# One mask pass and one r-by-decay pass for both chunks in units 0 to 8, the mix as two products of halves, and the opening in another order

## The chip, the core and the metric

The kernel runs on one core of one Trainium2 chip. The metric is the device time of one execution in microseconds (us). TensorE multiplies matrices, VectorE and ScalarE work element by element from SBUF or PSUM, GpSimd from SBUF alone, and SyncE issues the DMAs. In the views they are PE (PEld is its weight load), DVE, ACT, POOL and SP.

## The reference

Three stages follow each other. The first is a recurrence over time with one 48 by 48 state for each of 8 heads, for 4 batches of 768 steps. The second and third are two dense networks on the 3072 tokens that come out.

```python
for t in range(S):
    cur = einsum('bhd,bhe->bhde', u * k[t], v[t])
    y[t] = einsum('bhd,bhde->bhe', r[t], state + cur)
    state = w[t][..., None] * state + einsum('bhd,bhe->bhde', k[t], v[t])
x = y as 3072 x 384
h = x @ w_in;  x = (h * sigmoid(1.702 * h)) @ w_out          # 384 -> 2048 -> 384
h = x @ w_in2; s = h * softmax(h); x = layernorm(s) * g @ w_out2   # 384 -> 1024 -> 384
```

## The kernel before

**Units.** The recurrence is cut into 24 units (`NU`), six for each batch (`UB`), each of 128 time steps in two chunks of 64 (`C`). In a unit, rows 64 to 111 of the tile `rkw` hold chunk 0's 48 channels and rows 0 to 47 hold chunk 1's, for all heads side by side. The decays' running products are `P` (`f_scan`, token `F1`); `f_back` (`F3`) forms their inverses, and `f_k` (`F5`) multiplies them into k. `f_r1` (`F2` on GpSimd, `FV` on VectorE) multiplies r by the decay for chunk 1's rows into a tile R1, and `f_r0` (`FG` on GpSimd) does so for chunk 0's rows into R0.

**One unit on TensorE.** `scores` (`SA`) makes k times r within each chunk, 64 by 64 for each head: 16 products. `masked` (`M0`, `M1`) multiplies each chunk's scores by a triangular mask into the free half of R0 and R1. So R0 holds masked scores and decayed r one above the other, and `mix` (`X`) needs one product for each head and half chunk: 32 products, each 32 columns of weights wide, four of them beside each other, with v and the carried state stacked in the same way in `vs0` and `vs1`. `turn_k` (`ST`) and `copy_k` (`SK`) turn k, and `states` makes k times v. With tokens `DA`, `DB` it is added to the old state on TensorE by identity products, chunk by chunk; with `D` it stands alone, and `update` (`U1`, `U2`) adds on VectorE. A star at a token means the form on TensorE. `bonus`, `bonus_sum` and `bonus_mul` (`B`, then `BS`/`BR`, then `BV`/`BW`/`BX`) make the term with u; `total` (`V`) adds it. `turn`, `out_hi`, `out_lo` (`T`, `O`, `OL`) put the unit's output into the high and low parts that the dense stage reads.

**Banks.** A unit's PSUM is three banks of one set. In units 0 to 5 the scores fill bank 1, and the mix overwrites it. In units 6 to 8 scores of two half sets of heads lie in banks 2 and 0, the turned k in bank 1, and the mix in the rest of banks 2 and 0. Later units do as units 6 to 8, with the mix in bank 1.

**The dense stage and the order.** The first network's 16 weight slices come in as 64-bit numbers and are narrowed and split into a high and a low part (tokens `Lw`, `N0`, `N1` or `NA`, `N2`, `H`, `C`; `N1` is a VectorE shift and `NA` the same on ScalarE). `h`, `e`, `g`, `o` are rise, gelu, rest and fall of one token block and one slice: `h` and `o` are 9 products each, `h0`, `o0`, `h1`, `o1` of 256 tokens, `h9` and `o9` of 512. The order of everything in units 0 to 8 is the table `START`, written out by hand and run under a manual schedule, so that each engine takes its instructions in the table's order. From unit 9 on, the lists `ENTRY`, `BYPE` and `LONG` say which steps of a unit go behind which slice of the dense stage. After all 24 units the second network follows.

Of the kernel before, what the change touches and what calls it, by code (L numbers as in the profile page):

```python
# [990 lines left out]
```

## Time and profile before

| | us |
|---|---|
| median of 3 runs (lowest, highest) | 699.23 (696.68, 701.11) |
| profiled execution, its own time | 696.9 |
| its span, first to last instruction | 695.1 |
| TensorE busy in the span | 675.5 |
| VectorE, ScalarE, GpSimd busy | 516.7, 326.0, 151.2 |
| TensorE's last product of `START` ends, unit 9's `turn_k` begins | 134.35 |

The granted TensorE clock reads 1.00 in the whole span. A busy time is the union of an engine's instructions. Of TensorE's the ends are modelled, so a busy stretch can still hold short waits. The part of the span that the change touches is its first fifth: up to 134 us for units 0 to 8, and the handover to unit 9 behind it.

### The profile page before, as it was taken

What the parts mean: (1) busy time and instruction counts of PE and PEld (TensorE: products, weight loads), DVE (VectorE), ACT (ScalarE), POOL (GpSimd) and SP (SyncE); (2) the same over time, 40 slices, a digit from 0 to 9 for tenths busy, and PEclk for the clock granted to TensorE, in tenths of its full rate; (3) what the DMA queues carried; (4) which work ended last, traced back from release to release, by engine and by line L of the source; (5) the groups of instructions that cost most, each with busy time, mean ns of one, the idle gap of its engine ahead of it and who ended that gap; (6) DMA issues with size and microseconds to landing.
All of it is one profiled execution on the core that took longest, in us unless ns stands there. A gap on an engine that the chain in (4) does not pass through costs nothing.

```text
span 695.1 us, 15308 instructions
## 1 busy us (share of the span) xinstructions
PE 675.5 (97%) x6015; PEld 570.9 (82%) x6015; DVE 516.7 (74%) x815; ACT 326.0 (47%) x726; POOL 151.2 (22%) x146
## 2 busy tenths in 40 slices
PE   3899999999999999999999999999999999999997
PEld 2679878778888888888878888888899989999997
DVE  7898998898797777677777422566688888878872
ACT  4578985532334332432242224565655555455552
POOL 7555124332322222222123200120000000000000
PEclk9999999999999999999999999999999999999999
DMA  8696734545545455455453121340245444444443
GB/s 306 205 347 232 251 110 130 183 136 152 150 144 149 136 151 152 141 144 144 133 148 97 51 90 37 101 135 25 75 149 175 144 170 149 148 156 156 153 149 106
DMA packets 70872, 102.75 MB, mean 148 GB/s; under 512 B 16016, under 2 KB 55440, under 8 KB 70800
## 3 DMA queue, kind: packets, MB, share of 16 engines
q1 hardware_dynamic: 70656, 101.68, 46.0%
q8 instruction: 47, 0.77, 0.5%
q14 instruction: 25, 0.20, 0.1%
q10 hardware_dynamic: 144, 0.10, 0.0%
HBM read 77.82 MB, written 23.92 MB: 146 GB/s over the span
## 4 chain that ended last, share of the span: by engine, by line
PE 91%; DVE 3%; DMA 2%; ACT 2%; issue 1%; POOL 1%; SPq 0%; ACTq 0%; DVEq 0%; POOLq 0%
PE acc L628 26%; PE h L603 26%; PE o L739 14%; PE right L671 8%; PE left L671 7%; PE att L369 2%; DMA rk<-in_rkw 1%; PE att L279 1%; PE att L370 1%; PE d L525 1%; DVE xTl L420 1%; PE att L313 0%; PE att L317 0%; PE att L240 0%; PE att L306 0%
## 5 line engine op out<-in xcount | busy, mean ns | idle before, releaser
L628 PE MATMUL acc<-gh,w 128*128 128x512 f32 (+1 forms) x606 | 198.4, 384 | 0.0
L603 PE MATMUL h<-xTh,w 128*128 128x512 f32 (+1 forms) x606 | 164.9, 381 | 0.3 <-DVE gl L618 0.3
L611 ACT ACTIVATE gh<-h 128x512 fp32r<-128x512 f32 (+1 forms) x101 | 58.0, 575 | 212.6 <-PE h L603 211.0
L618 DVE TENSOR_TENSOR gl<-h,gh 128x512 fp32r<-128x512 f32 (+1 forms) x101 | 66.4, 659 | 87.3 <-ACT h L613 86.6
L628 PEld LDWEIGHTS acc<-gh,w 128*128 128x128 f32 x606 | 112.4, 188 | 22.5
L603 PEld LDWEIGHTS h<-xTh,w 128*128 128x128 f32 x606 | 110.0, 188 | 22.1 <-DVE gl L618 0.5
L628 PE MATMUL acc<-gl,w 128*128 128x512 f32 (+1 forms) x303 | 114.9, 379 | 0.0
L603 PE MATMUL h<-xTl,w 128*128 128x512 f32 (+1 forms) x303 | 82.4, 380 | 0.5 <-DVE xTl L420 0.5
L739 PE MATMUL o<-w,qh 128*128 128x384 f32 x384 | 70.9, 336 | 0.0
L739 PEld LDWEIGHTS o<-w,qh 128*128 128x128 f32 x384 | 67.7, 188 | 1.6
L603 PEld LDWEIGHTS h<-xTl,w 128*128 128x128 f32 x303 | 55.2, 188 | 12.4 <-DVE xTl L420 1.8
L628 PEld LDWEIGHTS acc<-gl,w 128*128 128x128 f32 x303 | 57.0, 188 | 10.1
L613 ACT ACTIVATE h<-h 128x512 f32<-128x512 f32 (+1 forms) x101 | 57.8, 572 | 0.0
L716 POOL TENSOR_TENSOR sm<-sm,mhalf 128x1 f32<-128x1 f32 x24 | 13.2, 549 | 199.0 <-DVE sm L715 177.6
L229 POOL TENSOR_TENSOR vd<-vd,dg 128x384 f32<-128x384 f32 x16 | 17.4, 1086 | 153.8 <-DMA vd<-in_vn 122.2
L173 POOL TENSOR_TENSOR R<-rk,P 64x512 f32<-64x512 f32 x22 | 29.0, 1317 | 73.9 <-PE att L370 42.2
L671 PE MATMUL right<-w,x2h 128*128 128x512 f32 x156 | 39.9, 391 | 0.0
L291 DVE TENSOR_TENSOR R<-att,cc 64x256 f32<-64x256 f32 (+1 forms) x82 | 36.8, 448 | 1.9 <-PE att L273 0.9
L739 PE MATMUL o<-w,ql 128*128 128x384 f32 x192 | 37.1, 334 | 0.0
L202 POOL TENSOR_TENSOR nr<-nr,nk 128x384 f32<-128x384 f32 x24 | 29.6, 1232 | 21.8 <-ACT nr L214 11.5
L188 DVE TENSOR_TENSOR_SCAN w<-w,ipc 112x520 f32<-112x520 f32 x24 | 33.5, 1397 | 0.8
L671 PE MATMUL left<-w,x2h 128*128 128x512 f32 x132 | 33.9, 392 | 0.0
(182 smaller groups left out, 1212.8 us busy)
## 6 DMA issues: line engine op xcount, KB each, us to landing
rk<-in_rkw SPq DMA_DIRECT2D x24, 512.0 KB, 4.1
d<-t SPq DMA_DIRECT2D x24, 512.0 KB, 2.6
back<-d SPq DMA_DIRECT2D x96, 128.0 KB, 2.7
x2b<-in_w SPq DMA_DIRECT2D x11, 768.0 KB, 6.0
w<-in_rkw SPq DMA_DIRECT2D x24, 261.0 KB, 3.0
nr<-in_nat SPq DMA_DIRECT2D x24, 192.0 KB, 2.9
nk<-in_nat SPq DMA_DIRECT2D x24, 192.0 KB, 2.9
vs<-in_vn SPq DMA_DIRECT2D x48, 96.0 KB, 4.1
```

The source lines that it names most:

```text
L173: (e or self.nc.gpsimd).tensor_tensor(out=heads(R1[0:64]), in0=heads(s["rkw"][0:64, 0:HC]), in1=heads(s["P"])[0:64, :, 0:C], op=ALU.mult)
L188: v.tensor_tensor_scan(out=w[:, n:0:-1], data0=w[:, n:0:-1], data1=self.ipc[:, n:0:-1], initial=0.0, op0=ALU.mult, op1=ALU.add)
L202: g.tensor_tensor(out=s["nr"], in0=s["nr"], in1=s["nk"], op=ALU.mult)
L229: g.tensor_tensor(out=heads(s["vd"]), in0=heads(s["vd"]), in1=dg.unsqueeze(2).to_broadcast([128, H, D]), op=ALU.mult)
L291: self.nc.vector.tensor_tensor(out=heads(R[q:q + 64])[:, h:h + n], in0=a, in1=m.unsqueeze(1).to_broadcast([64, n, C]), op=ALU.mult)
L603: nc.tensor.matmul(out=h_ps, lhsT=W1[f][:, ws + c * 128:ws + (c + 1) * 128], rhs=xs[:, c, tok], start=n == 0, stop=n == 8)
L611: nc.scalar.activation(out=gh, in_=h_ps, func=AF.Gelu_apprx_sigmoid)
L613: return nc.scalar.activation(out=h_ps, in_=h_ps, func=AF.Gelu_apprx_sigmoid)
L618: nc.vector.tensor_tensor(out=gl_, in0=g, in1=gh.bitcast(F32), op=ALU.subtract)
L628: nc.tensor.matmul(out=a, lhsT=W1[f][:, ws + e * 128:ws + (e + 1) * 128], rhs=gs, start=first and n == 0, stop=last and n == 2)
L671: nc.tensor.matmul(out=h_ps[:, b * 512:(b + 1) * 512], lhsT=xs[:, c], rhs=W2I[c][wb][:, b * 512:(b + 1) * 512], start=n == 0 and c == 0, s ...
L739: nc.tensor.matmul(out=o, lhsT=(lo if n == 2 else hi)[:, f * 128:(f + 1) * 128], rhs=W2O[f][n == 1], start=n == 0 and f == 0, stop=n == 2 ...
```

## The change

For units 0 to 8 (`QUADS` is now 9) four things are different.

1. `f_r1` multiplies all 112 rows in one pass, into one tile R0; `f_r0` is no longer called there.
2. Scores of both chunks lie one above the other in bank 1, and `masked` is one pass of 128 rows into a tile R1 of its own. Units 6 to 8 leave their four-fold layout and take that of units 0 to 5. `turn_k` uses bank 0 in every unit.
3. `mix` is two steps. `within` (token `X`) multiplies the masked scores by v, 16 products of 64 rows by 64 columns of weights. `mix` (token `Y`) adds r times the carried state, 16 products of 48 by 64.
4. `START` is a new table. Unit 3's states go from the TensorE form (`DA`, `DB`, starred `U1`, `U2`) to the VectorE form. The three `N1` become `NA`. `BX`, the bonus product on ScalarE, is left in unit 6 alone (before: units 4, 5, 6, 8). Unit 9's two r passes go to VectorE. In `ENTRY` unit 9's scores come after unit 8's mix.

```diff
-QUADS = UB
 LONE = 9
+QUADS = LONE
...
-    "turn+1 copy+1 scores+1 mix rk+3 w+3 v+2 total send vd+1 fetch masks+1",
+    "turn+1 copy+1 mix scores+1 rk+3 w+3 v+2 total send vd+1 fetch masks+1",
...
     def f_r1(self, i, e=None):
+        if i < QUADS:
+            n, r = 112, self.ap.tile([112, HC], F32, tag="R0", name=f"R0_{i}", bufs=2)
+            s["R0"] = r
...
     def masked(self, i, b):
         s, q = self.st[i], 64 * b
+        if i < QUADS:
+
+            R = s["R1"] = self.ap.tile([128, HC], F32, tag="R1", name=f"R1_{i}", bufs=2)
+            self.nc.vector.tensor_tensor(out=heads(R), in0=heads(s["A"]), in1=self.mask.unsqueeze(1).to_broadcast([128, H, C]), op=ALU.mult)
+            return
...
+    def within(self, i, e=None):
+
         mm, s = self.nc.tensor.matmul, self.st[i]
+        y, M = self.bank(i, 1)[:, 0:HD], s["R1"]
...
+        for h in range(H):
+            w, d = slice(h * C, (h + 1) * C), slice(h * D, (h + 1) * D)
+            mm(out=y[0:64, d], lhsT=M[0:64, w], rhs=s["vs0"][0:64, d], start=e is None and h == 0, stop=False)
+            mm(out=y[64:128, d], lhsT=M[64:128, w], rhs=s["vs1"][64:128, d], start=e is None and h == 0, stop=False)
+
+    def mix(self, i):
+        mm, s = self.nc.tensor.matmul, self.st[i]
+        if i < QUADS:
+
+            y, R = s["y"], s["R0"]
+            for h in range(H):
+                w, d = slice(h * C, (h + 1) * C), slice(h * D, (h + 1) * D)
+                mm(out=y[64:128, d], lhsT=R[0:48, w], rhs=s["vs1"][0:48, d], start=False, stop=h == H - 1)
+                mm(out=y[0:64, d], lhsT=R[64:112, w], rhs=s["vs0"][64:112, d], start=False, stop=h == H - 1)
+            return
...
-Lrkw:0 F1:0 F3:0 F5:0 FG:0 Ln:0 FV:0 SA:0 Lcst Lb:0 ST:0 B:0 BS:0 Lrkw:1 F1:1 F2:1 FG:1 M0:0 M1:0 La:0 SK:0 DA:0 Lw:1
+Lrkw:0 Ln:0 F1:0 F3:0 La:0 F5:0 Lcst B:0 Lrkw:1 F1:1 ST:0 SK:0 Lb:0 Lw:1 F3:1 BS:0 F2:0 SA:0 M0:0 F2:1 X:0 DA:0 Lw:0
```

VectorE, unit 0 and the start of unit 1, before (`rk` is k and r, `w` the decays, `R` the tiles R0 and R1):

```order
L195 TENSOR_TENSOR rk_110<-rk_110,w_108 112x512
L173 TENSOR_TENSOR R_0_125<-rk_110,P_112 64x512
L167 SCALAR_TENSOR_TENSOR P_166<-w_162,ind 112x520
L291 TENSOR_TENSOR R_0_119<-att_85,cc 64x512
L291 TENSOR_TENSOR R_0_125<-att_85,cc 64x512
L187 RECIPROCAL ipc<-P_166 112x8
L188 SCALAR_TENSOR_TENSOR w_162<-w_162,ipc 112x520
```

The same place after the change:

```order
L199 TENSOR_TENSOR rk_110<-rk_110,w_108 112x512
L166 SCALAR_TENSOR_TENSOR P_133<-w_129,ind 112x520
L191 RECIPROCAL ipc<-P_133 112x8
L192 SCALAR_TENSOR_TENSOR w_129<-w_129,ipc 112x520
L293 TENSOR_TENSOR R_0_175<-att_85,cc 128x512
L199 TENSOR_TENSOR rk_131<-rk_131,w_129 112x512
```

Unit 0's r pass (L173) has left VectorE, both scans of unit 1 stand ahead of unit 0's mask, and the mask is one instruction.

GpSimd at the same place, before (`nr`, `nk` are the bonus term's r and k, `cc` the constants, `vd` the bonus product):

```order
L179 TENSOR_TENSOR R_0_119<-rk_110,P_112 48x512
L202 TENSOR_TENSOR nr_121<-nr_121,nk_123 128x384
L203 TENSOR_TENSOR nr_121<-nr_121,cc 128x384
L173 TENSOR_TENSOR R_1_168<-rk_164,P_166 64x512
L179 TENSOR_TENSOR R_1_170<-rk_164,P_166 48x512
```

The same place after:

```order
L206 TENSOR_TENSOR nr_112<-nr_112,nk_114 128x384
L207 TENSOR_TENSOR nr_112<-nr_112,cc 128x384
L177 TENSOR_TENSOR R_0_157<-rk_110,P_116 112x512
L177 TENSOR_TENSOR R_1_177<-rk_131,P_133 112x512
L237 TENSOR_TENSOR vd_254<-vs_0_91,dg_148 64x384
```

Unit 0's r pass now stands behind the two bonus passes, the second of which reads the constants, and each unit has one pass instead of two.

ScalarE at the end of `START`, before (`x2a` is the dense stage's stored output, `vd` the bonus product of unit 8, `kTs` unit 9's turned k):

```order
L613 ACTIVATE h_0_1803<-h_0_1803 128x512
L638 ACTIVATE x2a<-acc_79 128x512
L638 ACTIVATE x2a<-acc_80 128x512
L638 ACTIVATE x2a<-acc_79 128x512
L227 ACTIVATE vd_1774<-vd_1774,dg_1765 128x48 x8
L245 ACTIVATE kTs_1888<-att_85 128x448
```

The same place after:

```order
L631 ACTIVATE h_0_1829<-h_0_1762 128x512
L656 ACTIVATE x2a<-acc_79 128x512
L656 ACTIVATE x2a<-acc_80 128x512
L656 ACTIVATE x2a<-acc_79 128x512
L249 ACTIVATE kTs_1857<-att_84 128x448
```

Unit 8's eight bonus instructions are gone from between the stores and the copy of unit 9's turned k.

## Rows read from the trace of the kernel before

**Rows 1.** The page's part 1: busy us, share, instructions of TensorE and VectorE.

```profile
PE 675.5 (97%) x6015; PEld 570.9 (82%) x6015; DVE 516.7 (74%) x815; ACT 326.0 (47%) x726; POOL 151.2 (22%) x146
```

**Rows 2.** Stretches of `START`: length; busy PE, PEld, DVE, ACT, POOL (xcount); PEclk, DMA share, GB/s.

```profile
0.00:30.40 30.40, 17.59 (x289) 12.94 (x289) 22.30 (x29) 14.41 (x51) 19.43 (x22) 1.00 0.72 254
30.40:56.90 26.50, 25.54 (x387) 21.17 (x387) 25.16 (x34) 20.50 (x64) 17.26 (x14) 1.00 0.80 277
56.90:134.40 77.50, 77.00 (x922) 63.32 (x921) 69.63 (x104) 55.47 (x165) 25.92 (x22) 1.00 0.56 182
```

**Rows 3.** The chain of waits in order of time, 42 to 47 us: start, us, what.

```profile
42.37 1.02 ACT x2b L488
...
43.41 1.54 DVE wf L490
44.95 1.15 DVE P L167
46.10 0.46 DVE xTl L420
```

**Rows 4.** VectorE, 0 to 135 us, by line and shape: count, busy, mean ns, idle.

```profile
L618 DVE TENSOR_TENSOR gl<-h,gh 128x512 fp32r<-128x512 f32 x11 | 7.5, 686 | 0.3 <-ACT h L613 0.2
L291 DVE TENSOR_TENSOR R<-att,cc 64x512 f32<-64x512 f32 x10 | 6.9, 689 | 1.1 <-PE att L273 0.9
...
L291 DVE TENSOR_TENSOR R<-att,cc 64x256 f32<-64x256 f32 x12 | 5.1, 421 | 0.2
...
L173 DVE TENSOR_TENSOR R<-rk,P 64x512 f32<-64x512 f32 x2 | 2.1, 1073 | 0.0
```

**Rows 5.** GpSimd, 0 to 135 us, the r passes by line and shape.

```profile
L179 POOL TENSOR_TENSOR R<-rk,P 48x512 f32<-48x512 f32 x10 | 13.5, 1346 | 17.0 <-DMA nk<-in_nat 7.9 <-DVE P L167 3.9 <-DMA rk<-in_rkw 3.1
...
L173 POOL TENSOR_TENSOR R<-rk,P 64x512 f32<-64x512 f32 x8 | 11.0, 1374 | 21.7 <-DVE P L167 13.7 <-PE acc L322 5.7 <-PE att L240 2.1
```

**Rows 6.** VectorE's timeline: the same f_k pass in units 0 and 5.

```profile
6.35 1.48 DVE L195 TENSOR_TENSOR rk<-rk,w 112x512 f32<-112x512 f32 x1
...
87.11 0.69 DVE L195 TENSOR_TENSOR rk<-rk,w 112x512 f32<-112x512 f32 x1
```

**Rows 7.** TensorE's timeline: first product of a step, first of the next.

```profile
9.29 0.36 PE L273 MATMUL att<-R,rk 48*64 48x64 f32 x1 [0.91 <-DVE R L173]
...
48.22 0.53 PE L313 MATMUL att<-vs,cc 112*48 112x192 f32 x2
49.49 0.39 PE L628 MATMUL acc<-gh,w 128*128 128x256 f32 x1
...
54.19 0.23 PE L369 MATMUL att<-vs,R 112*32 112x48 f32 x1
55.01 0.38 PE L628 MATMUL acc<-gh,w 128*128 128x256 f32 x1
...
63.98 0.24 PE L305 MATMUL att<-vs,kTs 64*48 64x48 f32 x1
64.38 0.23 PE L273 MATMUL att<-R,rk 48*64 48x64 f32 x1
...
91.34 0.27 PE L272 MATMUL att<-R,rk 48*64 48x64 f32 x1
92.42 0.50 PE L628 MATMUL acc<-gh,w 128*128 128x512 f32 x1
...
102.35 0.27 PE L279 MATMUL att<-R,rk 48*64 48x64 f32 x1
102.98 0.50 PE L628 MATMUL acc<-gh,w 128*128 128x512 f32 x1
```

**Rows 8.** Timelines at the handover to unit 9: ScalarE, VectorE, TensorE.

```profile
134.55 1.58 ACT L638 ACTIVATE x2a<-acc 128x512 f32<-128x512 f32 x3 [1.69 <-PE acc L628]
...
137.94 0.56 DVE L377 TENSOR_TENSOR vd<-att,vd 128x384 f32<-128x384 f32 x1 [1.27 <-ACT vd L227]
...
153.57 0.24 PE L305 MATMUL att<-vs,kTs 64*48 64x48 f32 x1 [1.29 <-ACT kTs L261]
```

More of the change, by code (lines that the diff above doesn't have):

```diff
@@ L237, in turn_k @@
         kt, s = self.st[i]["kt"], self.st[i]
-        s["kT"] = self.bank(i, 0 if i < QUADS else 1)
+        s["kT"] = self.bank(i, 0)
         for p in range(4):
@@ L265, in scores @@
         mm, s = self.nc.tensor.matmul, self.st[i]
-        kt, R0, R1 = s["kt"], s["R0"], s["R1"]
+        kt, R0 = s["kt"], s["R0"]
         if i < QUADS:
-            A = self.bank(i, 1)
-            s["A"] = [[(A[0:64], 0, H)], [(A[64:128], 0, H)]]
+            A = s["A"] = self.bank(i, 1)
             for h in range(H):
@@ L272, in scores @@
                 mm(out=A[0:64, c], lhsT=kt[64:112, c], rhs=R0[64:112, c], start=True, stop=True)
-                mm(out=A[64:128, c], lhsT=kt[0:48, c], rhs=R1[0:48, c], start=True, stop=True)
+                mm(out=A[64:128, c], lhsT=kt[0:48, c], rhs=R0[0:48, c], start=True, stop=True)
             return
+        R1 = s["R1"]
         P, Q = self.bank(i, 2)[:, 0:4 * C], self.bank(i, 0)[:, 0:4 * C]
@@ L350, in update @@
         v.tensor_tensor(out=dst, in0=kv, in1=pc, op=ALU.mult)
-    def mix(self, i, e=None):
+    def within(self, i, e=None):
         mm, s = self.nc.tensor.matmul, self.st[i]
-        one = e is None
-        if i < QUADS or i >= LONE:
-            s["y"] = y = self.bank(i, 1)[:, 0:HD]
-            y = [y[:, h * D:(h + 1) * D] for h in range(H)]
-        else:
-            s["y"] = y = self.bank(i, 3).rearrange("p (b c) -> p b c", b=2)[:, :, 4 * C:4 * C + 4 * D]
-            y = [y[:, h // 4, (h % 4) * D:(h % 4 + 1) * D] for h in range(H)]
-        if e is not None:
-            mm(out=s["y"], lhsT=self.ident, rhs=s["vd"], start=True, stop=False)
+        y, M = self.bank(i, 1)[:, 0:HD], s["R1"]
+        s["y"] = y
+        if e is not None:
+            mm(out=y, lhsT=self.ident, rhs=s["vd"], start=True, stop=False)
+        for h in range(H):
[11 more added lines that the diff above has]
+            return
+        y = s["y"] = self.bank(i, 1)[:, 0:HD]
         for h in range(H):
@@ L786, in rwkv_moe_moe2 @@
         ST=at.turn_k, SK=at.copy_k, SA=at.scores, M0=lambda i: at.masked(i, 0), M1=lambda i: at.masked(i, 1),
-        D=at.states, DA=lambda i: at.states(i, 0), DB=lambda i: at.states(i, 1), U1=lambda i, e=None: at.update(i, 0, e), U2=lambda i, e=None: at.update(i, 1, e), X=at.mix, V=at.total,
+        D=at.states, DA=lambda i: at.states(i, 0), DB=lambda i: at.states(i, 1), U1=lambda i, e=None: at.update(i, 0, e), U2=lambda i, e=None: at.update(i, 1, e), X=at.within, Y=at.mix, V=at.total,
         T=at.turn, O=lambda i: at.out_hi(i, X), OL=lambda i, e=None: at.out_lo(i, X, e),
```

49 lines of the change are left out of this document (24 added, 25 removed).

## The prediction

> **What bounds the kernel now.** I read the page first: TensorE is busy for 675.5 of the 695.1 us [rows 1], so whatever lengthens TensorE's work late in the kernel lengthens the kernel. Then I cut `START` into stretches at two marks of the program, unit 1's turned output (30.4 us) and unit 3's (56.9 us), and read the engines in each [rows 2]. In the first 30.4 us TensorE is busy for 17.59 us only: this is a chain from engine to engine. From 30.4 to 56.9 us TensorE is busy 25.54 of 26.5 us and VectorE 25.16 us, so the two bound it together, and the chain of waits shows how: at 42 us it leaves TensorE for a weight conversion on ScalarE, a narrowing pass, a scan and an output split on VectorE, and comes back with unit 3's turn of k [rows 3]. From 56.9 to 134.4 us TensorE is busy 77.00 of 77.5 us and VectorE 69.63 us: here TensorE's work alone sets the end, and a faster VectorE or GpSimd has 0.5 us to win. After 134 us nothing of the change runs but the handover to unit 9.
>
> So the question is how much TensorE work the change adds behind 56.9 us, and how much earlier that mark is reached.
>
> **VectorE and GpSimd lose work.** A pass over 128 rows of 512 costs what one over 64 rows does: 686 ns against 689 ns [rows 4]. So the single mask pass takes about 0.69 us, and saves 0.69 us in each of units 0 to 5 and 4 x 0.42 - 0.69 = 1.0 us in each of units 6 to 8: 7.1 us in `START`, of which 2.8 us lie in the opening (units 0 to 3). Unit 0's r pass leaves VectorE as well, one of two passes of mean 1.07 us [rows 4]. Against that stand two more state additions of unit 3 and one weight shift less in the opening, all of about half a pass, which I set to nothing. VectorE has some 3.9 us less to do up to the mark. GpSimd's r passes cost 1346 ns for 48 rows and 1374 ns for 64 [rows 5], so one of 112 rows should cost about 1.36 us too, and the 18 passes before become 7. That is 15 us of GpSimd, an engine whose work lies beside others'; its worth is indirect. The f_k pass took 1.48 us in unit 0, beside a GpSimd r pass, and 0.69 us in unit 5 [rows 6].
>
> The Trainium skill (SBUF — State Buffer, section "Who interferes with whom") says that VectorE with two SBUF inputs and GpSimd share one port pair, which the first holds for its whole instruction while the other waits. The two rows of f_k agree. By the rule alone, the three GpSimd passes that go from the opening could give VectorE back up to their whole length, 3 x 1.36 = 4.1 us in place of the 0.8 us taken below, and the sum at the end would be about nothing instead of +3.2 us.
>
> I take from this row at most 0.8 us for each of three GpSimd passes that are gone from units 0 to 3, and expect a third of it, 0.8 us, since most VectorE passes of the opening are not stretched.
>
> **TensorE gains work.** The mix before takes 55.01 - 54.19 = 0.82 us for 32 products, four beside each other [rows 7]. After it is 16 products of `within` and 16 of `mix`, which can stand only two beside each other, since each covers 64 columns of weights. No row shows this form. The nearest are the scores, with the same width and places, but 64 columns moved instead of 48: 92.42 - 91.34 = 1.08 us [rows 7]. From below the old mix bounds it, whose 16 groups of two would take twice its eight groups of four in a pure count; each half then costs the whole old mix, 0.82 us. I take 0.9 us for a half, nearer to the 0.82 us because its 48 moved columns are the same. Behind the mark stand five `within` (units 4 to 8) and four `mix` (4 to 7), and before stood four old mixes: 9 x 0.9 - 4 x 0.82 = +4.8 us (4.1 to 6.4 at the ends). Unit 8's old mix and its new second half stand behind `START` alike.
>
> The scores of units 6 to 8 also go from four to two beside each other: from 102.98 - 102.35 = 0.63 us to 1.08 us [rows 7], three times: +1.35 us. The turn of unit 4's k slips behind the mark: +0.3 us. Unit 3's states lose two identity forms of 49.49 - 48.22 = 1.27 us and take one of 64.38 - 63.98 = 0.40 us [rows 7]: -2.1 us on TensorE, all ahead of the mark.
>
> **The opening.** Unit 0's first pair of scores had both r passes at 9.29 us [rows 7], because GpSimd and VectorE made one each. Now the single pass waits on GpSimd behind two bonus passes, and the second of these reads the constants, whose DMA is issued after two loads of v. I reckon its end near 11 us. TensorE turns k in the meantime, which it did afterwards before, so unit 0 loses about 1 us, not 2. What is queued behind that wait on TensorE is all of unit 0; on VectorE it is the one mask pass, with unit 1's scans already done ahead of it. Up to unit 1's turned output I see no net change: the order has then done two products' worth more (unit 2's scores, one split) in a stretch where TensorE is idle for 12.8 of 30.4 us. Between the marks TensorE has unit 3's identities and that earlier work less (-2.1 -1.1 -1.75), and four halves for two mixes more (+2.0), and one fall moved from ahead of the mark to just behind it, which I count in (+1.1): about -2 us. VectorE has about -3 us there. The two bound it together, so the mark comes 2 to 3 us earlier; I take 2.5 us. It is nothing if unit 0's delay goes through to the end, +2 us at worst, and -6 us if VectorE's 3.9 us and the stretched passes all count.
>
> **The handover.** Unit 8's total waited 1.27 us for its bonus product on ScalarE, and TensorE later 1.29 us for unit 10's k, which goes through VectorE's queue behind that total [rows 8]. The eight bonus instructions are gone, so I expect the 1.29 us to go. But unit 9's scores now need the bank of its turned k, so they wait for its copy, and this stands on ScalarE behind the stores of 1.58 us [rows 8] with only unit 8's `mix` to cover it: about +1.0 us. Together -0.3 us. The 0.5 us of idle time behind the mark may go too: -0.5 us.
>
> **Sum.** -2.5 (opening) + 4.8 (halves) + 1.35 (scores) + 0.3 (turn) - 0.3 (handover) - 0.5 (idle) = +3.2 us, since TensorE stays full behind it. The profiled execution took 696.9 us (span 695.1), 2.3 us under the median of the three runs; the sum goes 696.9 + 3.2 = 700.1 for such an execution, and 699.2 + 3.2 = 702.4 for the median.
>
> **Rivals.** *The halves do not stand beside each other.* If the two products of a pair, which read different rows and write the same bank, took turns, a half would cost twice the 0.64 us that 0.82 has without its start, 1.3 to 1.5 us: nine times +0.5 behind the mark and seven times ahead of it, where TensorE is 96% busy, so +8 us on top: 710 us. Against it: the scores write one bank from different rows and start in pairs, 1.08 us for 16. The point from which it decides is a half above 1.2 us. The Trainium skill (TensorEngine Tiling (Array Packing), section "Gotcha 1: PSUM Pressure") says that different row tiles cannot access the same PSUM bank at once, which is this rival. The scores' rows do not bear it out, so I give it one chance in ten.
>
> *The opening gives nothing.* Unit 0's r pass behind the bonus passes and the constants delays the chain by 1 to 2 us, and the order-bound queues of VectorE (a total that waits for a bonus product, with unit 1's second update behind it) keep it: 3.2 + 2.5 + 1.5 = +7.2 us, 706.4 us. For it: the first stretch is a chain with 12.8 us of idle TensorE.
>
> *The late stretch is not TensorE's.* If its busy time hides waits for VectorE, which is 90% busy there, then VectorE's 4.3 us less in masks there pay for the new products, and the +4.8 and +1.35 us fall away: 3.2 - 6.15 = -3 us, 696.2 us. Against it: the idle time there is 0.5 us.
>
> *The opening gives much more.* Units 0 to 3 reach the mark 10 us or more earlier, with all waits for conversions gone: 692 us or less. TensorE's own work up to the mark speaks against it.
>
> **Chances.** My case (698 to 706.2) 0.48; the late stretch not TensorE's (693 to 698) 0.16; the opening gives nothing 0.16, a little over half of it above 706.2; the halves apart 0.10; the opening much faster 0.10. A difference under 1%, 7 us, is about what a measurement of this kernel cannot tell from no change. So faster by over 1%: 0.10; within 1%: 0.48 + 0.16 + 0.07 = 0.71; slower by over 1%: 0.19. The range from 692.5 to 710 leaves out the fast case and half of the halves apart.
>
> **What would show it.** In the profile after: a `within` or `mix` of 0.8 to 1.1 us, pairs starting together; one mask pass of 0.69 us; first scores near 11 us; unit 3's turned output and the fall moved behind it done by 54 to 55 us; unit 9's turn of k at 137 to 139 us instead of 134.35; no wait for unit 10's k, but one of about 1 us for unit 9's scores. The prediction is wrong if unit 9's turn comes before 134 us, or if TensorE shows idle time of several us between the mark and there.

## The result and the profile after

The changed kernel takes 703.94 us (median of 18 runs, 702.27 to 708.09), the kernel before beside it 698.05 us (18 runs, 695.81 to 703.02): a ratio of 1.0094, interval 1.0073 to 1.0115. So it is 5.9 us slower by the medians, and 6.6 us by the ratio. The 18 times lie in two groups, twelve from 702.27 to 704.58 and six from 706.38 to 708.09; the profiled execution is the 702.27, with a span of 700.5 us, 5.4 more than before.

The page after, busy times, against [rows 1]:

```profile
PE 682.2 (97%) x6007; PEld 580.1 (83%) x6007; DVE 508.1 (73%) x801; ACT 323.6 (46%) x705; POOL 135.9 (19%) x140
```

TensorE has 6.7 us more, VectorE 8.6 us and GpSimd 15 us less. The windows after, cut at unit 1's turned output, at the end of the fall behind unit 3's, and at unit 9's turn of k, against [rows 2] (columns: stretch, length, busy time of each engine, granted clock, DMA share, GB/s):

```profile
0.00:30.90 30.90, 18.53 (x321) 14.74 (x321) 20.06 (x27) 16.89 (x53) 14.81 (x22) 1.00 0.82 290
30.90:56.10 25.20, 23.92 (x342) 20.84 (x343) 22.04 (x31) 19.41 (x64) 8.94 (x8) 1.00 0.82 281
56.10:140.50 84.40, 84.29 (x957) 70.74 (x956) 67.66 (x96) 53.41 (x150) 23.36 (x21) 1.00 0.49 162
```

The third row is where the time went: 84.4 us instead of 77.5, and TensorE is busy in 84.29 of them. VectorE fell from 69.63 to 67.66 us there, and it did not help. The marks themselves, in TensorE's timeline, first before (turned output of unit 3, first product behind it, turn of unit 9's k), then after (the same, and unit 9's scores):

```profile
56.57 0.49 PE L400 MATMUL att<-cc,vd 128*128 128x128 f32 x3
56.82 0.36 PE L628 MATMUL acc<-gh,w 128*128 128x256 f32 x1
...
134.35 0.55 PE L240 MATMUL att<-cc,rk 112*128 112x112 f32 x4
```

```profile
54.73 0.49 PE L418 MATMUL att<-cc,vd 128*128 128x128 f32 x3
...
56.13 0.40 PE L621 MATMUL h<-xTh,w 128*128 128x256 f32 x2
...
140.50 0.55 PE L244 MATMUL att<-cc,rk 112*128 112x112 f32 x4
...
142.76 0.27 PE L283 MATMUL att<-R,rk 48*64 48x64 f32 x1 [0.65 <-ACT kTs L249]
```

In the changed order one fall stands behind unit 3's turned output that stood ahead of it before, so the mark after is 56.13 us, the end of that fall, against 56.82 us; the same rises and falls lie ahead of both. With these marks the 5.4 us split into three: -0.7 up to the mark, 84.37 - 77.53 = +6.84 behind it, and -0.75 in the rest of the span (560.0 against 560.75). The wait of 1.29 us for unit 10's k [rows 8] is not there, and one of 0.65 us for unit 9's scores is.

A `within` of unit 5 and a `mix` of unit 6, from TensorE's timeline (L370 and L371 are a pair of `within`, L380 and L381 one of `mix`):

```profile
91.16 0.25 PE L370 MATMUL att<-vs,R 64*64 64x48 f32 x1
91.17 0.25 PE L371 MATMUL att<-vs,R 64*64 64x48 f32 x1
...
91.91 0.24 PE L314 MATMUL att<-vs,kTs 64*48 64x48 f32 x1
...
92.58 0.50 PE L621 MATMUL h<-xTh,w 128*128 128x512 f32 x1
...
114.20 0.25 PE L380 MATMUL att<-vs,R 48*64 48x48 f32 x1
114.21 0.25 PE L381 MATMUL att<-vs,R 48*64 48x48 f32 x1
114.29 0.22 PE L380 MATMUL att<-vs,R 48*64 48x48 f32 x1
...
115.27 0.60 PE L244 MATMUL att<-cc,rk 112*128 112x112 f32 x4
```

The products of a pair start 0.01 us apart, so they stand beside each other; the second pair comes 0.08 us later, each further one 0.06 us. A `mix` takes 115.27 - 114.20 = 1.07 us. A `within` takes 0.75 us up to the first product of the states, which overlap it and then take 0.67 us, where those of units 5 to 8 alone took 0.50 in the kernel before.

The mask pass and the r passes, by source line (duration shortest, median, longest in ns):

```profile
L293 DVE TENSOR_TENSOR R<-att,cc x8: 658/680/692, 13.9 to 132.7; 128x512 f32<-128x512 f32 x8
...
L177 POOL TENSOR_TENSOR R<-rk,P x21: 1171/1192/2125, 9.3 to 378.2; 64x512 f32<-64x512 f32 x14, 112x512 f32<-112x512 f32 x7
```

0.68 us on VectorE as reckoned, and about 1.19 us on GpSimd, a little less than the 1.36 us taken. Unit 0's chain, from the timelines of GpSimd, VectorE and TensorE:

```profile
9.33 1.17 POOL L177 TENSOR_TENSOR R<-rk,P 112x512 f32<-112x512 f32 x1
...
10.55 0.36 PE L275 MATMUL att<-R,rk 48*64 48x64 f32 x1 [1.20 <-POOL R L177]
...
11.87 2.08 DVE L192 TENSOR_TENSOR_SCAN w<-w,ipc 112x520 f32<-112x520 f32 x1
13.87 0.66 DVE L293 TENSOR_TENSOR R<-att,cc 128x512 f32<-128x512 f32 x1
...
14.59 0.34 PE L370 MATMUL att<-vs,R 64*64 64x48 f32 x1 [2.06 <-DVE R L293]
```

First scores come at 10.55 us, and then TensorE waits 2.06 us for the mask, which stands on VectorE behind unit 1's back scan, itself late and stretched to 2.08 us.

One thing had escaped the reading of the profile before: TensorE's pace. Scores of unit 1, first in the kernel before, then in the changed one:

```profile
20.54 0.31 PE L272 MATMUL acc<-R,rk 48*64 48x64 f32 x1
20.64 0.31 PE L272 MATMUL acc<-R,rk 48*64 48x64 f32 x1
```

```profile
18.27 0.36 PE L275 MATMUL acc<-R,rk 48*64 48x64 f32 x1
...
18.43 0.25 PE L275 MATMUL acc<-R,rk 48*64 48x64 f32 x1
...
18.53 0.22 PE L275 MATMUL acc<-R,rk 48*64 48x64 f32 x1
18.59 0.22 PE L275 MATMUL acc<-R,rk 48*64 48x64 f32 x1
```

In the kernel before all products up to 22.3 us are at the slow pace (here 0.31 us, a step every 0.10), in the changed one those up to 18.4 us (after that 0.22 us, every 0.06). The column of the granted clock reads 1.00 for both.

### The profile page after: what moved, and what is told of

Same layout as the page of the kernel before. It is cut to its first block, busy times and chain, and to the rows that moved or that the text cites. A ratio compares the mean times of both kernels' runs of the same rounds, so it can differ in the third digit from the quotient of the medians.

```text
span 700.5 us, 15235 instructions
## 1 busy us (share of the span) xinstructions
PE 682.2 (97%) x6007; PEld 580.1 (83%) x6007; DVE 508.1 (73%) x801; ACT 323.6 (46%) x705; POOL 135.9 (19%) x140
## 4 chain that ended last, share of the span: by engine, by line
PE 93%; DVE 2%; DMA 1%; issue 1%; ACT 1%; SPq 1%; POOL 1%; ACTq 0%; DVEq 0%; POOLq 0%
PE acc L646 28%; PE h L621 27%; PE o L757 14%; PE right L689 8%; PE left L689 6%; PE att L389 1%; PE att L370 1%; PE att L283 1%; DMA w<-in_rkw 1%; PE att L275 1%; PE att L380 1%; PE d L543 1%; PE att L244 0%; PE att L390 0%; PE att L315 0%
## 5 line engine op out<-in xcount | busy, mean ns | idle before, releaser
L233 POOL TENSOR_TENSOR vd<-vd,dg 128x384 f32<-128x384 f32 x17 | 18.4, 1079 | 158.1 <-DMA vd<-in_vn 128.0
L177 POOL TENSOR_TENSOR R<-rk,P 64x512 f32<-64x512 f32 (+1 forms) x21 | 26.4, 1258 | 80.7 <-PE att L390 42.5
L166 DVE TENSOR_TENSOR_SCAN P<-w,ind 112x520 f32<-112x520 f32 x24 | 32.6, 1358 | 4.4 <-DMA w<-in_rkw 4.0
L689 PEld LDWEIGHTS right<-w,x2h 128*128 128x128 f32 x156 | 29.1, 188 | 5.6
```

The costliest lines, as they stand in the source:

```text
L166: self.nc.vector.tensor_tensor_scan(out=P, data0=s["w"][:, 0:H * PW], data1=self.ind[:, 0:H * PW], initial=0.0, op0=ALU.mult, op1=ALU.add)
L177: (e or self.nc.gpsimd).tensor_tensor(out=heads(r[0:n]), in0=heads(s["rkw"][0:n, 0:HC]), in1=heads(s["P"])[0:n, :, 0:C], op=ALU.mult)
L233: g.tensor_tensor(out=heads(s["vd"]), in0=heads(s["vd"]), in1=dg.unsqueeze(2).to_broadcast([128, H, D]), op=ALU.mult)
L689: nc.tensor.matmul(out=h_ps[:, b * 512:(b + 1) * 512], lhsT=xs[:, c], rhs=W2I[c][wb][:, b * 512:(b + 1) * 512], start=n == 0 and c == 0, s ...
```

## The experiments

The table holds, for the profiled execution of each kernel, the mark (the first product behind the fall that follows unit 3's turned output; in the old order of before, e2 and w3, where that fall stands ahead, the first product behind the turned output itself), the stretch from there to unit 9's turn of k, and when TensorE's products reach the fast pace (in w1 to w3 they start at it, fall, and reach it again at this time; in e10 they fall once more from 40 to 43.4 us), all from TensorE's timelines; and the ratio to the kernel before with its interval. The changed kernel's own ratio is 1.0094, and 0.001 is 0.7 us.

| kernel | fast pace from | mark | stretch behind | ratio |
|---|---|---|---|---|
| before | 22.3 | 56.82 | 77.53 | 1 |
| changed | 18.4 | 56.13 | 84.37 | 1.0094 (1.0073 to 1.0115) |
| e1, mix 1 of 8 | 20 | 56.56 | 81.87 | 1.0054 (1.0035 to 1.0073) |
| e3, halves of 32 columns | 24 | 57.49 | 83.30 | 1.0076 (1.0054 to 1.0097) |
| e4, old mix late | 20 | 56.75 | 85.13 | 1.0125 (1.0097 to 1.0154) |
| e6, the same, v later | 28.1 | 60.84 | 80.59 | 1.0044 (1.0021 to 1.0068) |
| e5, opening | 17 | 54.33 | 84.35 | 1.0050 (1.0030 to 1.0070) |
| e8, e6 and e5 | 25.6 | 58.33 | 79.12 | 0.9998 (0.9976 to 1.0020) |
| e10, old form, new order | 23, and again 43.4 | 58.10 | 80.43 | 1.0041 (1.0025 to 1.0057) |
| e7, e6 with four-fold scores | 27.8 | 60.38 | 85.40 | 1.0133 (1.0103 to 1.0163) |
| e2, new form, old order | 30.7 | 67.79 | 89.68 | 1.0337 (1.0311 to 1.0363) |
| w1, changed, warm | 26.4 | 59.09 | 84.38 | 1.0085 (1.0059 to 1.0111) |
| w2, e8, warm | 23.5 | 56.42 | 79.12 | 0.9983 (0.9967 to 0.9999) |
| w3, before, warm | 22.5 | 58.24 | 78.15 | 0.9993 (0.9977 to 1.0008) |

### The stretch behind the mark: is it TensorE's own work?

**Seven eighths of four halves left out.**

```diff
-            for h in range(H):
+            for h in range(H - 1 if 4 <= i < 8 else 0, H):
```

> Units 4 to 7 compute the carried half of the mix (`mix`) for one head of eight only, so the carried state's part of seven heads is left out of their outputs; all other work and the order are those of the changed kernel. Seven eighths of four halves of 1.06 us are 3.7 us of TensorE work behind unit 3's turned output; less a fixed start that stays. My theory (the late stretch is TensorE's own work): 2.9 to 3.7 us faster than the changed kernel, unit 9's turn of k near 137 us instead of 140.5. Rival (VectorE or another engine sets that stretch and the halves lie beside its work): within 0.7 us of the changed kernel, with new idle time on TensorE.

The stretch became 2.5 us shorter and the time about 2.8 us (1.0054 against 1.0094), just under the 2.9 to 3.7 us of the theory and far from the rival's 0.7. Three of the four halves fell from 1.07 to 0.25 us, 2.46 us together. The fourth gave nothing, since TensorE then waits for unit 7's split on VectorE, its only wait between the mark and 140 us:

```profile
PE att L244 <- DVE xTl L438: 0.9, 1, 0.9
```

So work taken from TensorE shortens that stretch by its full length, until the next engine in line shows.

**Halves of 32 columns, four beside each other.**

```diff
-                mm(out=y[64:128, d], lhsT=R[0:48, w], rhs=s["vs1"][0:48, d], start=False, stop=h == H - 1)
...
+                for t in (0, 32):
+                    w = slice(h * C + t, h * C + t + 32)
+                    mm(out=y[64 + t:96 + t, d], lhsT=R[0:48, w], rhs=s["vs1"][0:48, d], start=False, stop=h == H - 1, tile_position=(0, 64 + t))
```

> Each half of the mix in units 0 to 8 as 32 products with 32 columns of weights, four beside each other, instead of 16 with 64 columns, two beside each other. Same arithmetic. Theory (the width of the pair sets the step, 0.058 us for two products, while four narrow ones took 0.82 us for 32 in the mix before): a half takes 0.80 to 0.85 us instead of 1.06, nine of them behind the mark give 1.9 to 2.3 us, so the kernel is about 2 us faster than the changed one. Rival (the count of products or the rows read set the step, not how many stand beside each other): a half takes 1.0 us or more, the time within 0.5 us of the changed kernel or above it.

A half standing alone takes 0.82 us (`mix` of unit 6 from 114.95 to its follower at 115.77), as the theory had it:

```profile
114.95 0.23 PE L384 MATMUL att<-vs,R 48*32 48x48 f32 x1
114.96 0.23 PE L385 MATMUL att<-vs,R 48*32 48x48 f32 x1
...
115.77 0.60 PE L244 MATMUL att<-cc,rk 112*128 112x112 f32 x4
```

But the stretch gained 1.07 us, not 2: `within` with its states went only from 1.42 to 1.32 us, and unit 7's half waits for the split as above. On the clock the difference, some 1.3 us, is inside the intervals. The price of a half goes with the layout, the width of the weights and how many products stand beside each other, which change together here; it does not go with the count of products, which doubled.

**The old mix from unit 4 on.** Units 4 to 8 with two r passes, two masks and one mix of 32 products; their scores stay as changed.

```diff
+HALVES = 4
...
-        if i < QUADS:
+        if i < HALVES:
...
+        if HALVES <= i < QUADS:
+            self.f_r0(i, e or self.nc.gpsimd)
```

> Units 4 to 8 go back to two r passes (same engine), two mask passes and one mix of 32 products, four beside each other; their scores stay two beside each other, units 0 to 3 and the order stay as in the changed kernel. Theory (TensorE alone counts behind the mark): five within and four mix of 1.06 us go, four old mixes of 0.82 us come, 9.5 - 3.3 = 6.2 us less TensorE work, so 4.5 to 6.2 us faster than the changed kernel, though VectorE has five mask passes (3.4 us) and GpSimd five r passes (6 us) more. Rival (the late stretch is VectorE's or GpSimd's as well): 1 us faster at most, or slower, with TensorE waiting for the second mask pass.

It was slower than the changed kernel, by about 2 us, so the theory seemed to fall. The waits of SyncE's queue and the windows show a cause of its own:

```profile
SPq L153 <- PE att L401: 7.1, 1, 7.1
```

```profile
80.00:88.00 8.00, 8.00 (x83) 6.44 (x71) 3.55 (x6) 2.17 (x4) 3.17 (x4) 1.00 0.68 211
88.00:96.00 8.00, 6.47 (x58) 5.03 (x57) 5.54 (x7) 6.94 (x22) 2.83 (x3) 1.00 0.78 283
```

Unit 6's load of v (L153) overwrites v rows that unit 4 used. In the changed kernel `within` has read those rows 15 us before `mix`; the old mix reads all rows at the later place. So the load waited 7.1 us for it, the weight loads queued behind it came late, ScalarE waited for them (2.17 us busy of 8), VectorE for ScalarE, and TensorE last. The halves have a use that the forecast did not name: they release v early. The next run tests this cause.

**The same with that load behind the next loads.**

```diff
-NA:12 N2:12 e9:6 h9:8 Lv:4 B:5 BS:5 g9:6 H:9 C:10 BW:4 Y:4 La:6 V:4 Ln:6 C:9 Lw:15 N0:11 ST:5 e9:8 o9:6 NA:11 T:4 g9:8
-O:4 N0:15 SK:5 h9:7 e9:7 NA:15 H:12 Lrkw:6 Lw:13 N2:11 B:6 H:11 OL:4 F1:6 SA:5 h9:9 g9:7 o9:8 M0:5 X:5 D:5 C:11 N2:15
+NA:12 N2:12 e9:6 h9:8 Lv:4 B:5 BS:5 g9:6 H:9 C:10 BW:4 Y:4 V:4 Ln:6 C:9 Lw:15 N0:11 ST:5 e9:8 o9:6 NA:11 T:4 g9:8
+O:4 N0:15 SK:5 h9:7 e9:7 NA:15 H:12 Lrkw:6 Lw:13 N2:11 B:6 H:11 OL:4 La:6 F1:6 SA:5 h9:9 g9:7 o9:8 M0:5 X:5 D:5 C:11 N2:15
```

> The run with the old mix in units 4 to 8, once more, with unit 6's load of v moved behind the next r, k and weight loads in SP's queue. In that run this load waited 7.1 us for unit 4's mix, since the old mix reads the v rows that the changed kernel's within has long read, and the weight loads behind it came late; TensorE was idle for 4 to 5 us around 95 us. Theory (TensorE alone counts behind the mark, once that wait is gone): 5.8 us less TensorE work between unit 3's fall and unit 8's last fall, less waits of up to 2 us for VectorE, which has 3.4 us of masks more: 3.5 to 5.8 us faster than the changed kernel, so 0 to 2.5 us slower than the kernel before. Rival (VectorE and GpSimd bound that stretch too, the load was only one of several): less than 2 us faster than the changed kernel, with TensorE waiting for mask or r passes in several units.

The stretch went from 84.37 to 80.59 us and the ratio from 1.0094 to 1.0044, 3.5 us, the lower end of the theory. Against e4 it is 5.7 us (1.0125 to 1.0044), so the load's wait was what had cost e4 its gain. Of the 5.6 us that the products are shorter by, 1.4 us went into the wait for unit 7's split, behind VectorE's masks and its r passes of units 5 and 7. With the second of these r passes on GpSimd (in e8 below, which also has e5's opening) that wait is 0.4 us and the stretch 79.12 us. That is the kernel before's 77.53 us plus 3 x 0.46 = 1.4 us for the two-fold scores of units 6 to 8, and 0.2 us. So 5.25 of the 6.84 us behind the mark were undone by runs; the 1.4 us of the scores rest on their rows (1.08 against 0.62 us) and the sum, since the run that was to undo them, the next, can't be used.

**Four-fold scores in units 6 to 8 as well.**

```diff
-QUADS = LONE
+QUADS = 6
-        s["kT"] = self.bank(i, 0)
+        s["kT"] = self.bank(i, 1 if QUADS <= i < LONE else 0)
```

> The run e6 with the scores of units 6 to 8 four beside each other again, in two banks, their masks in four passes of 256 columns, their mix in another bank, as in the kernel before. So only units 0 to 3 and the order are the change's. Theory (TensorE sets the end): three scores of 0.62 instead of 1.08 us, 1.35 us less TensorE work, so 0.7 to 1.4 us faster than e6 and near the kernel before or up to 1 us under it. Rival (VectorE's 0.9 us more of masks is what counts by then): within 0.5 us of e6 or slower.

The ratio is 1.0133 (1.0103 to 1.0163): slower than e6, as the rival has it, but not by VectorE's 0.9 us. In this order unit 6's turned k lands in the bank where unit 5's mix still lies, so that unit 5's total adds the former. The scores fell to 0.62 us, but TensorE has five waits between the mark and unit 9's turn of k, 1.8 us twice, all for VectorE, and its granted clock is 0.50 from 133.5 to 136.5 us behind one of the two. The order was written for two-fold scores; this says nothing on TensorE's price, and it is not used.

### The opening: why 0.7 us and not 2.5?

**Unit 0's chain first.**

```diff
-Lrkw:0 Ln:0 F1:0 F3:0 La:0 F5:0 Lcst B:0 Lrkw:1 F1:1 ST:0 SK:0 Lb:0 Lw:1 F3:1 BS:0 F2:0 SA:0 M0:0 F2:1 X:0
+Lrkw:0 Lcst F1:0 F3:0 F2:0 F5:0 Ln:0 La:0 B:0 Lrkw:1 F1:1 ST:0 SA:0 SK:0 Lb:0 Lw:1 M0:0 F3:1 BS:0 F2:1 X:0
```

> The changed kernel with unit 0's chain in another order: the constants loaded first after r, k and w of unit 0, unit 0's r pass on GpSimd ahead of its bonus passes, its mask on VectorE ahead of unit 1's back scan. Nothing else changes. Theory (the opening's gain of 2.5 us was lost because unit 0's first scores and its mask stand behind other work: TensorE waits 2.06 us for the mask and starts late, and then works at half pace for longer): first scores 1 to 2 us earlier than 10.55, X:0 without a wait for the mask, full pace 1 to 2 us earlier than 18.3, unit 3's turned output 1.5 to 2 us earlier than 54.73, and the kernel 1 to 2 us faster than the changed one. Rival (VectorE and the loads of the first 55 us bound the opening as a whole, so unit 0's lead is absorbed): T:3 within 0.5 us of 54.73, the time within 0.7 us of the changed kernel.

1.0050 instead of 1.0094: 3.1 us faster, a little more than expected. First scores at 8.83 us, and `within` at 12.51, still behind a wait for the mask:

```profile
12.51 0.34 PE L370 MATMUL att<-vs,R 64*64 64x48 f32 x1 [1.70 <-DVE R L293]
```

Unit 3's turned output comes at 52.93 instead of 54.73, and the stretch behind is 84.35 us as in the changed kernel: a start that is 1.8 us earlier goes through to unit 9 in full. The edit moves three things at once (constants, r pass, mask), and which of them gave it was not separated. Behind unit 9 the two profiled executions differ the other way: here TensorE waits 1.35 us for unit 10's k, in the changed kernel it does not, and the rest of the span is 561.57 us against 560.00. So the profiled spans differ by 0.2 us only. One of the six times here is late, of the changed kernel's eighteen six (told of below); this mixture is part of the 3.1 us, and how much was not measured.

**The new form in the old order.** Each `within` just ahead of its unit's states, each `mix` where the old one stood.

```diff
+Lrkw:0 F1:0 F3:0 F5:0 F2:0 Ln:0 SA:0 Lcst Lb:0 ST:0 B:0 BS:0 Lrkw:1 F1:1 F2:1 M0:0 La:0 SK:0 X:0 DA:0 Lw:1 N0:1 NA:1
+F3:1 U1:0* DB:0 F5:1 BV:0 Y:0 SA:1 ST:1 N2:1 U2:0* Ln:1 Lw:0 N0:0 V:0 B:1 NA:0 SK:1 M0:1 Lrkw:2 Lb:1 N2:0 H:0 La:1 X:1
```

> The new products, the one mask pass and the one r pass, in the order that START had before (the r pass of unit 0 on GpSimd ahead of its bonus passes, constants loaded late, each within just ahead of the states). This tells the structure from the rewritten order. Theory one (the cost is the structure's, behind the mark, and the rewritten order gave next to nothing): within 2 us of the changed kernel, so 4 to 8 us slower than the kernel before; first scores at 9.5 us or earlier instead of 10.55. Rival one (the rewritten order costs the time, by unit 0's late r pass and mask): 3 us or more faster than the changed kernel, near the time before. Rival two (the rewritten order is what made the structure bearable): 3 us or more slower than the changed kernel.

722.9 us, 1.0337 (1.0311 to 1.0363): rival two. First scores were early (8.77 us) and yet the kernel is some 17 us slower than the changed one. In the profiled executions the mark comes 11.7 us later than in the changed kernel, the stretch behind is 5.3 us longer and the rest 4.6 us. Ahead of the mark TensorE waits for unit 3's mask, and its granted clock falls (windows of that stretch, and the product behind the wait):

```profile
52.00:55.00 3.00, 0.64 (x6) 0.43 (x4) 2.95 (x5) 2.47 (x19) 0.00 (x0) 1.00 0.88 307
55.00:60.00 5.00, 4.96 (x56) 3.98 (x57) 0.68 (x2) 3.49 (x6) 3.93 (x4) 0.51 0.44 167
```

```profile
55.04 0.34 PE L370 MATMUL att<-vs,R 64*64 64x48 f32 x1 [2.40 <-DVE R L293]
```

Behind 2.4 us without work, 0.51 is TensorE's lower level, 1.2 of 2.4 GHz. Its products also kept the slow pace up to 30.7 us, and behind a wait of 1.94 us for unit 9's turned k the clock fell once more (0.62 granted in 160.5 to 165 us). How the 17 us divide between pace and waits is open.

**The old form in the new order** is the fourth corner.

```diff
-HALVES = 4
+HALVES = 0
```

The edit is against e6, with unit 6's load of v moved as there; the scores stay two-fold in all units.

> All of units 0 to 8 with two r passes (both on GpSimd where the changed kernel makes one there), two mask passes and the old mix of 32 products at the place of the carried half, in the changed kernel's order of START. It is the fourth corner of a square with the kernel before (old form, old order), the changed kernel (new form, new order) and the run of the new form in the old order, which was 25 us slower than the kernel before. Theory (form and order belong together, and the new order without the new form loses what VectorE and GpSimd no longer do): the opening is slower, T:3 at 57 to 61 us instead of 54.73, the late stretch as short as before, so 0 to 5 us slower than the kernel before. Rival (the order alone is what helps the opening and the form only costs): T:3 at 54 to 55.5 us and the time 1 to 3 us below the kernel before.

1.0041: 3 us slower than the kernel before, as the theory had it. Its marks were a little off: unit 3's turned output came at 56.70 us, just ahead of the 57 to 61, and the stretch behind is 80.43 us, not as short as before (77.53), with the two-fold scores and waits in it. So the new order costs the old form 3 us and saves the new form 17; the new form costs 24 us in the old order and 4 in the new one. Form and order can't be judged apart. One comparison more: e10 and e6 differ in the form of units 0 to 3 alone, and their ratios are 1.0041 and 1.0044. That the new form gains anything in the opening, where TensorE waits, is therefore not shown on the clock (e6's early times lie some 2 us under e10's, its late ones some 3 us over them).

**Seven products ahead of everything.** The slow pace in the opening suggested work for TensorE while it waits for the first loads. In three kernels, seven products of 384 columns on constants, whose result nobody reads:

```diff
+        for _ in range(7):
+            nc.tensor.matmul(out=at.bank(0, 1)[:, 0:384], lhsT=at.ind[:, 0:128], rhs=at.ind[:, 0:384], start=True, stop=True)
         for t in order:
```

> The changed kernel, with seven products of 384 columns on constants ahead of everything on TensorE; they run while it waits for the first loads, and nobody reads their result. Theory (the opening is lost by TensorE's pace: its first products step at half the later pace, to 18.3 us in one profiled execution and to 28 us in another of the same opening, and this makes two groups of times some 4.5 us apart): the products of units 0 and 1 step at full pace from the first or nearly, first mask some 1 us earlier, unit 3's turned output 2 to 3 us earlier than 54.73, only one group of times left, median 3 to 4.5 us under the changed kernel's. Rival (loads and VectorE set the opening, and the two groups come from elsewhere): the marks move by under 0.7 us, and both groups stay.

1.0085 against 1.0094: no gain that can be measured, so the theory fell. The windows of w1:

```profile
2.00:9.80 7.80, 7.15 (x18) 4.01 (x18) 4.24 (x6) 1.24 (x5) 3.42 (x6) 1.00 0.98 325
9.80:11.20 1.40, 0.00 (x0) 0.00 (x0) 1.33 (x3) 0.96 (x9) 1.40 (x2) 1.00 1.03 420
11.20:12.40 1.20, 1.13 (x32) 1.01 (x32) 1.11 (x1) 1.10 (x10) 1.20 (x2) 1.00 1.03 415
12.40:13.20 0.80, 0.02 (x2) 0.00 (x0) 0.74 (x2) 0.47 (x1) 0.80 (x1) 0.86 1.00 409
13.20:20.00 6.80, 6.79 (x107) 5.90 (x108) 2.85 (x4) 3.86 (x5) 4.94 (x5) 0.50 0.85 286
```

Unit 0's turn and scores do run at the fast pace (a product of the scores 0.22 instead of 0.31 us). But TensorE then idles 1.4 us for the r pass and 0.8 us for the mask, and the clock is granted at 0.50 (1.2 GHz) from there to some 26 us, with TensorE busy all the time. In this execution the slow stretch was moved, not removed, and the mark came at 59.09, 3 us later than in the changed kernel's.

> The run e8_best with the same seven products ahead. Theory (TensorE's pace in the opening): 1.5 to 3 us faster than e8_best and one group of times, so 1 to 3 us under the kernel before. Rival: within 0.7 us of e8_best.

> The kernel before with the same seven products ahead. Theory (TensorE's pace in the opening costs the kernel before as well, whose products step at half pace to 22.28 us): 1.5 to 4 us faster than the kernel before, unit 1's turned output before 29 us instead of 30.43. Rival (its chain in the opening is set by loads, VectorE and GpSimd): within 0.7 us.

On the kernel before the seven products do nothing that can be measured (0.9993, 0.9977 to 1.0008); unit 1's turned output stays at 30.46 us, the rival's case.

**A version that joins what helped.** e8 is e6 with e5's opening and the second r pass of units 4 to 8 always on GpSimd; w2 adds the seven products.

```diff
-            self.f_r0(i, e or self.nc.gpsimd)
+            self.f_r0(i, self.nc.gpsimd)
```

> Units 4 to 8 with the old mix, two r passes (the second on GpSimd) and two masks, with unit 6's v load moved, and the opening of the run e5: the new form only where VectorE and GpSimd bound the kernel (units 0 to 3). Theory (the two effects add: 3.9 us less from unit 3's fall to unit 8's last fall, in trace rows, and some 1.8 us less up to it): 5.5 to 6.5 us faster than the changed kernel, 697 to 698.5, so within 1 us of the kernel before; with the two r passes that leave VectorE's queue the 1.4 us wait for unit 7's split may shrink as well, which would take it under the kernel before. Rival (the late stretch then waits for VectorE, so an earlier start is lost there): over 700.

The effects add as expected: e8 stands level with the kernel before (0.9998, 0.9976 to 1.0020), w2 just ahead of it (0.9983, 0.9967 to 0.9999), at a median of 695.68 us against 697.78. Neither is a clear win over the kernel before; against the changed kernel both win some 7 us. What the seven products give is not settled by w2: its median is 1.8 us under e8's (697.47), the ratios differ by 1.0 us within their intervals, and three of its twelve times are still late (698.04 to 699.23, the others up to 696.14).

**The two groups of times.** The changed kernel, e1, e4 and e6 have the same instructions and the same order on TensorE up to unit 4. In the first three profiles the fast pace comes by 20 us and the mark at 56.13 to 56.75 us. In e6 the slow pace lasted to 28.1 us:

```profile
27.19 1.09 PE L555 MATMUL d<-w,neg 128*128 128x384 f32 x1
28.08 0.70 PE L247 MATMUL acc<-cc,rk 112*128 112x112 f32 x4
28.71 0.25 PE L381 MATMUL acc<-vs,R 64*64 64x48 f32 x1
...
60.84 0.40 PE L632 MATMUL h<-xTh,w 128*128 128x256 f32 x2
```

Its mark is 4.7 us later than the changed kernel's, which is about the distance between the groups: e6's times are 698.39 to 700.18 five times and 703.57 to 704.10 four times, and this profile is one of the latter (704.02). The profile of e7, which has the same products up to unit 4 too, shows the same: fast pace from 27.8 us, mark at 60.38. So the six late ones of the changed kernel are likely executions whose pace rose late; none of them was profiled. What decides it in an execution was not settled. It is not the only source of a late time. e8's profiled execution (702.38, where e8's lowest is 695.12) has a TensorE wait of 1.76 us for unit 10's k, and behind it the granted clock falls to the lower level:

```profile
159.00:162.40 3.40, 3.40 (x37) 2.73 (x24) 3.37 (x6) 0.37 (x1) 1.18 (x1) 0.50 0.23 82
```

Behind unit 9's turn this execution takes 563.10 us, that of w2, with the same work there and no such fall, 560.71.

## Why the prediction held, and what was mis-sized

The forecast was 702.4 us with a range of 692.5 to 710; 703.94 came. The mechanism was right: the end is set by TensorE's work behind the mark, and VectorE's and GpSimd's relief buys nothing there. The size was less so than the times look: +3.2 us was forecast and +5.9 measured (+5.4 in the profiled executions). That the times lie 1.5 us apart is in part luck, since the kernel before came out at 698.05 beside it and not at the 699.23 that the forecast started from. Term by term, in the profiled executions:

| term | predicted | measured |
|---|---|---|
| opening | -2.5 | -0.7 |
| five `within`, four `mix`, for four old mixes | +4.8 | +5.6 |
| scores of units 6 to 8 | +1.35 | +1.4 |
| turn of unit 4's k | +0.3 | +0.3 |
| idle time behind the mark | -0.5 | -0.4 |
| handover and the rest | -0.3 | -0.75 |

**The halves.** A `within` costs 0.75 + 0.67 - 0.50 = 0.92 us net of its states, a `mix` 1.07: 5 x 0.92 + 4 x 1.07 - 4 x 0.82 = 5.6 us. The 0.9 us was taken near the lower bound because of its 48 moved columns; the row of the scores, at the upper bound (1.08 us), was the right one for a half, and a `within` comes near 0.9 us only because the states overlap it. Width and place of the weights set the step, not the columns moved (48 here, 64 in the scores), as the run with 32 columns showed (0.82 us).

**The halves do not stand beside each other** was refuted by the first pair in the timeline and by the 1.07 us, which lie below the 1.2 us from which this rival was to decide. By the Trainium skill (TensorEngine Tiling (Array Packing), section "Gotcha 1: PSUM Pressure") different row tiles cannot access one PSUM bank at the same time; here pairs from different rows, writing different partitions of one bank, start 0.01 us apart at every step, so the rule does not hold for them as it stands.

**The opening** was the term with the largest error, -0.7 us instead of -2.5. Up to unit 1's turned output, where no net change was forecast, it lost 0.50 us (30.93 against 30.43). From there to the mark it gained 1.19 us (25.20 against 26.39). In that stretch VectorE has 3.0 us less to do, as forecast, and TensorE 1.5 us where about 2 was forecast, and TensorE's waits grew by 0.3 us. The 2.5 us were taken between the relief of the two engines; by these rows VectorE's did not count, as in the late stretch.

The delay of unit 0 was forecast well at its first scores: 10.55 us where near 11 was said, 1.26 us behind the 9.29 us at which the first pair with both r passes stood before. Not foreseen was the wait of 2.06 us for the mask behind them (the mask was said to have unit 1's scans "already done ahead of it"; the load of unit 1's decays let the first scan begin at 10.32 us only, and the back scan ended at 13.95). Unit 0's turned output came 0.38 us earlier than before all the same (26.35 against 26.73). TensorE's pace rose at 18.4 instead of 22.3 us, which no term held and which may have hidden part of the delay. e5 shows that an earlier start of unit 0 goes on to the mark and to unit 9. For the opening alone the rival *the opening gives nothing* was nearer than its chance of 0.16 says. Of the signs named ahead, the mark (54 to 55 us) and unit 9's turn of k (137 to 139 us) were missed, at 56.13 and 140.50 us.

**The late stretch is not TensorE's**: refuted by e1, e6 and e8. Its grain of truth is unit 7's split, where VectorE is next in line: TensorE waited 0.4 to 1.4 us for it in e1, e3, e6 and e8.

**The handover** gave a little more than was said, but not for the reason given. The wait of 0.65 us for unit 9's scores is there, forecast at 1.0. The wait for unit 10's k was to go because unit 8's total no longer waits for its bonus product. That total did come earlier behind unit 9's turn of k (1.73 us behind it instead of 3.59), but VectorE turned unit 10's k no earlier (145.77 - 134.35 = 11.42 us before, 151.90 - 140.50 = 11.40 after), since it waits 1.56 us in between for a gelu. These are VectorE's turn of unit 10's k before and after, and TensorE's wait in e5:

```profile
145.77 0.71 DVE L250 STREAM_TRANSPOSE x2b<-rk 128x512 f32<-128x512 f32 x1
```

```profile
151.90 0.71 DVE L254 STREAM_TRANSPOSE x2b<-rk 128x512 f32<-128x512 f32 x1
```

```profile
158.85 0.24 PE L314 MATMUL att<-vs,kTs 64*48 64x48 f32 x1 [1.35 <-ACT kTs L265]
```

TensorE comes there 0.9 us later behind unit 9's turn (9.24 against 8.34 us at unit 9's states), and in the profiled execution the way of k through memory to ScalarE's copy took 6.0 us instead of 6.4. Together they take up the wait. In e5, with the same instructions there, that way took 7.3 us and the wait was back with 1.35 us. So this part of the term came out in part by the luck of the execution.

## What to carry to other kernels

Before trading product count for fewer element-wise passes, ask which engine ends the stretch: here 0.69 us of VectorE per unit was bought with about 1.2 us of TensorE, a loss where TensorE is full; that it is a gain where TensorE waits is not shown (e6 against e10). Price a new product form by the nearest form in width and place of its weights, not in moved columns. When a tile is read by two smaller products instead of one, look at what its early release lets a load queue do, and test an undo together with the loads that it holds up.

## What the runs showed of the hardware

The granted clock's column says nothing of TensorE's level until the first change: it reads 1.00 at the start of every plain run, while a product of the scores takes 0.31 us there and 0.22 us later, and the same two durations go with granted clocks of 0.50 and 1.00 in w1. So the slow pace in the openings is taken for the lower level by the duration, not by the column. By the Trainium skill (TensorE: Matmul & The Clock Gate, section "Part 1: The HAM clock gate (the "warmup" mystery)") the array runs at 1.2 GHz by default and at 2.4 GHz once it has been kept busy, and events of that gate in a trace are not to be trusted alone; the durations here agree with both.

In w1 the clock fell behind gaps of 1.4 and 0.8 us with 1.1 us of scores between, after 7.15 of 7.8 us busy. It fell later in other kernels too, behind single waits: 2.40 us in e2, 1.84 us in e10 and in e7, 1.76 us in e8, and read 0.50 to 0.51 for 3 to 7 us after them. There a gap cost twice, once as waiting and once as pace.
